# Two in-place token sums of a gate/up pass, issued behind the first pair's evictions

## The chip, the cores and the metric

The kernel runs on one core of one Trainium2 chip. The metric is the device time of one execution in microseconds (us). A profiled execution gives, beside that, a span: from the first to the last instruction of the program. The engines are TensorE (PE, the matmuls), VectorE (DVE), ScalarE (ACT), GpSimd (POOL) and SyncE (SP), which here only issues DMA transfers. Each engine works through its own queue in program order; an instruction can wait for semaphores that other engines or transfers raise, and everything behind it in its queue waits with it.

## What is computed

Two layers, each a linear-attention block and a gated MLP, on 2048 tokens of 1024 features; the MLP has 3584 inner features. The MLP, where the change lies:

```python
def _B_ref(x, w_gate, w_up, w_down):
    g = jnp.einsum("bsd,df->bsf", x, w_gate)
    u = jnp.einsum("bsd,df->bsf", x, w_up)
    h = g * u
    return jnp.einsum("bsf,fd->bsd", h, w_down)
...
x = x + _A_ref(_layernorm(x, axis=-1), A_wqkv, A_wo)
x = x + _B_ref(_layernorm(x, axis=-1), B_w_gate, B_w_up, B_w_down)
```

and the same two lines once more for the second layer, with the same weights.

## The kernel before

The MLP of a layer runs in two passes of 1024 tokens. Each has a gate/up part (`gateup`, with 14 pairs) and a down part (`down`). A pair `p` is a block of 256 inner features, once of the gate weights (unit A, `c = 0`) and once of the up weights (unit B, `c = 1`). Both units multiply a 1024x256 weight block with the tokens of the pass, and do so with seven block products instead of eight: the tokens (features by tokens, in float16) and the weights are cut into two by two blocks, sums of blocks are formed on VectorE, and products 1 to 7 of sums are added up in PSUM. One product is four matmuls of 128x128 by 128x512 (`pe`, line 1591). The token blocks that enter products 1 and 5 are `xblk(0, s0)`, a part of the normalized tokens, and the sum `T1`.

Products 1 and 5 are themselves split into seven half-size products (matmuls of 128x128 by 128x256, line 1661), from pair 1 on. Those take further sums of sub-blocks of the tokens (`tp_ops`) and of the weights (`sums0`). Four token sums belong to each of the two products. Three of them go to buffers of their own. The remaining one is formed in place: the quarter `b12` of the block is overwritten with `b22 - b12`. Pair 0 of the first layer's first pass is not split: its products 1 and 5 read the whole block, `b12` included. So in this pass the in-place sum is held back (`XD["1"]`, `XD["5"]`, line 906) until pair 0 has read the block.

What runs when is written out by hand. `ORDERS[(False, 0)]` is a list of tokens, gone through once for each pair; a `+` means the next pair, a `'` the pair before:

```python
(False, 0): "S1+ D2A M3B' P5A T1 P1B R0 P7A 57 P6B S5+ M5A D4A M2A 11+ P7B D3A 16+ D2B M4A P5B M3A R1 T0+ M2B M5B 51+ D4B P1A+ 56+ 17+ D3B P6A+ M4B",
```

`P1B` is product 1 of unit B and so on; `D2`, `D3`, `D4` are products that finish a PSUM bank. `M5A` and `M5B` evict the bank of product 5: `mul0` (line 1766) copies it on ScalarE (line 1771), and for unit B two VectorE sums follow, an addition of 128x1024 and a multiplication of 128x512. The other M tokens evict the other banks; `M4B` and `M2B` are scaled evictions on VectorE (line 843). `11`, `16`, `17` are the stages of split product 1, `51`, `56`, `57` those of split product 5: each issues half-size matmuls, then `seed` (line 1677, ScalarE) and `join` (line 1680, VectorE). `S1` and `S5` are the four weight sums for a pair's split products. `T0` and `T1` are ticks: they store weight sums and form the next ones (`prep_s`, four sums of 128x2x512), run a step of a layer norm (line 506 on VectorE, a transposing transfer at line 591 on SyncE), and every second pair `wd_load` (a load of raw down weights), `wd_prep` (its four sums of 128x1024, behind the load) and `wd_store`. `R0` and `R1` issue the load of a later weight block.

`emit` turns a token into instructions. It issues the in-place sums directly behind the last product that reads the block, `P1B` or `P5B`. All sums of this kind are recorded by `tt` at line 840, so the profile shows them under that line, and the matmuls under line 1591 or 1661. Dependencies are found by the recorder from the byte ranges that each instruction reads and writes. A matmul group of `pe` and a half-size one declare the whole token block as read.

Of the kernel before, what the change touches and what calls it, by code (L numbers as in the profile page):

```python
# [180 lines left out]
def build_kernel(nc, A_x, A_wqkv, A_wo, B_w_gate, B_w_up, B_w_down, out):  # L181
# [152 lines left out]
    with ExitStack() as es:  # L334
# [86 lines left out]
        def R(o, n):  # L421
            return [(o, o + n)]

        def r_x(i, lo=0, hi=D):
            return [(O_X + (i * D + lo) * 2, O_X + (i * D + hi) * 2)]
# [13 lines left out]
        def dma(dst_ap, src_ap, wr, key, rd=()):  # L439
            P.add("sp", lambda e: e.dma_start(dst_ap, src_ap), rd=rd, wr=wr, dma_sem=key)  # L440
# [279 lines left out]
        XD = {}  # L720
# [24 lines left out]
        def pass_base(first, ps_):  # L745
            return ps_ * (NU + len(d_units(first, 0)))
# [125 lines left out]
        def x_pop(n=1):  # L872
            for _ in range(n):
                if XQ:
                    XQ.pop(0)[1]()
# [6 lines left out]
        def x_need(tk):  # L882
            lab = X_NEED.get(tk[:2])
            while any(k == lab for k, _ in XQ):
                x_pop()
# [34 lines left out]
        def prep_s(n):  # L920
            a, b = sorted([(n + 1) % NR, (n + 2) % NR])
            ring = [f(O_SLOT, NR * SZ_SLOT // 2).rearrange("p (s x) -> p s x", s=NR)[:, a:b + 1:b - a] for f in (vb, vh)]

            def w(h, c):
                return ring[0][:, :, 1024 * h:1024 * h + 1024].rearrange("p s (k c) -> p s k c", c=256)[:, :, :, 128 * c:128 * c + 128]

            def rg(lo, hi):
                return r_slot(n, lo, hi) + r_slot(n + 1, lo, hi)
            sv = [ring[1][:, :, 2048 + 512 * i:2560 + 512 * i].rearrange("p s (k c) -> p s k c", c=128) for i in range(4)]
            a11, a12, a21, a22 = w(0, 0), w(1, 0), w(0, 1), w(1, 1)  # L930
            ra = rg(0, 4096)
            rs = [rg(4096 + i * 1024, 5120 + i * 1024) for i in range(4)]
            tt(sv[0], a21, a22, ALU.add, ra, rs[0])
            tt(sv[1], sv[0], a11, ALU.subtract, ra + rs[0], rs[1])
            tt(sv[2], a11, a21, ALU.subtract, ra, rs[2])
            tt(sv[3], a12, sv[1], ALU.subtract, ra + rs[1], rs[3])

        def store_s(n):
            u = split_n(n)[1]
            sl = (n + 1) % NR  # L940
            dma(wscr[u], vh(r_slot(n)[0][0] + 4096, 2048), R(V_S + u * 32, 32), KSW[sl], rd=r_slot(n, 4096, 8192))
# [608 lines left out]
        def pro_step(pro, n):  # L1550
            for _ in range(n):
                k = len(P.streams["pe"])
                while pro and len(P.streams["pe"]) == k:
                    pro.pop(0)()

        def layer_B(lnp, nxt, first):
# [236 lines left out]
            def gateup(ps_, ticks, l2):  # L1793
                jit = first and ps_ == 0
                NP = NU // 2
                pairs = [pair(ps_, p, "" if jit and p == 0 else l2) for p in range(NP)]

                order = ORDERS[not first, ps_].split()
                n0 = pass_base(first, ps_)

                def emit(it, tk):
                    off = {"'": -1, "+": 1}.get(tk[-1], 0)
                    tk = tk.rstrip("'+=")
                    p = it + off
                    if tk[0] == "R":
                        if it > 0 or (it == 0 and tk == "R1"):
                            ring_issue()
                        return
                    if not 0 <= p < NP:
                        return  # L1810
                    c, x = pairs[p], "AB".find(tk[-1])
                    if jit and tk[0] not in "PDMFT" and tk[-1] not in c["L"] and tk[0] not in c["L"]:
                        return
                    if p < 2:
                        x_need(tk)
                    if p == 0:
                        if tk[0] in "PDM":
                            x_pop()
                    if tk[0] == "P":
                        c["p" + tk[1]](x)  # L1820
                        if jit and p == 0 and tk in ("P1B", "P5B"):
                            XD[tk[1]]()
                    elif tk[0] == "D":
                        c["fin"](tk[1], x)
                    elif tk[0] == "M":
                        c["c22"](x) if tk[1] == "5" else c["fmul"](tk[1], x)
                    elif tk[0] == "S":
                        if jit:
                            c["sums0"](tk[1])
                        else:  # L1830
                            c["sums"](SPG[tk[1] == "5"], "make" if first else "load")
                    elif tk[0] == "F":
                        c["fold"]()
                    elif tk[0] == "T":
                        i = int(tk[1])
                        if jit:
                            if i == 0:
                                store_s(n0 + 2 * p)
                                store_s(n0 + 2 * p + 1)
                            elif p + 1 < NP:  # L1840
                                prep_s(n0 + 2 * p + 2)
                        ticks(2 * p + i)
                    else:
                        c["L"][tk[0]]["st" + tk[1]]()

                seq = [(it, tk) for it in range(-1, NP) for tk in order
                       if tk[0] == "R" or 0 <= it + {"'": -1, "+": 1}.get(tk[-1], 0) < NP]
                early = ("11", "16", "17", "P1", "21", "26", "27", "31", "36", "37", "S1", "S5", "T0", "T1", "Ra", "Rb")
                npro = [tk[:2] in early for _, tk in seq].index(False)
                if jit:  # L1850
                    npro = 1
                    seq.insert(0, seq.pop([tk for _, tk in seq].index("P1A+")))
                pro = [(lambda x=x: emit(*x)) for x in seq[:npro]]

                def tail():
                    for tk in order:
                        if tk[-1] == "'":
                            emit(NP, tk)
                    ring_issue()
                    if "Ra" in order:  # L1860
                        ring_issue()
                    for t in range(1 if jit else 3, 8):
                        i = 8 * ps_ + t
                        dma(x_res[:, i, :], xscr[i * 128:(i + 1) * 128, :], r_x(i), KX[i], rd=R(V_X + i * 32, 32))

                def run():
                    pro_step(pro, len(pro))
                    for x in seq[npro:]:
                        emit(*x)
                    return tail  # L1870
                return pro, run
# [523 lines left out]
```

## Time and profile before

| | us |
|---|---|
| median of 3 runs | 1436.92 |
| lowest and highest run | 1436.63, 1437.53 |
| the profiled execution | 1439.2 |
| its span | 1437.5 |
| gate/up of the first pass, about | 238 to 405 |

The profile is one execution. A row of its timeline has the start in us from the span's start, the duration in us, the engine and line, the operation with output and input shapes, the number of instructions merged into the row, and, in brackets, how long the engine stood idle before it and what released it. Instructions of one engine overlap a little, so rows may start before the row above has ended. All buffers lie in one SBUF tensor, `arena`, and the PSUM banks in `ps`, so names tell little and shapes and lines tell more. In the table of waits a row has the waiting instruction, whom it waited for, the total in us, the number of waits and the longest.

### The profile page before, as it was taken

What the parts mean: (1) busy time and instruction counts of PE and PEld (TensorE: products, weight loads), DVE (VectorE), ACT (ScalarE), POOL (GpSimd) and SP (SyncE); (2) the same over time, 40 slices, a digit from 0 to 9 for tenths busy, and PEclk for the clock granted to TensorE, in tenths of its full rate; (3) what the DMA queues carried; (4) which work ended last, traced back from release to release, by engine and by line L of the source; (5) the groups of instructions that cost most, each with busy time, mean ns of one, the idle gap of its engine ahead of it and who ended that gap; (6) DMA issues with size and microseconds to landing.
All of it is one profiled execution on the core that took longest, in us unless ns stands there. A gap on an engine that the chain in (4) does not pass through costs nothing.

```text
span 1437.5 us, 22075 instructions
## 1 busy us (share of the span) xinstructions
PE 1422.7 (99%) x8248; PEld 801.1 (56%) x8304; DVE 1141.0 (79%) x2048; ACT 700.3 (49%) x1478; POOL 226.0 (16%) x265
## 2 busy tenths in 40 slices
PE   9999999999999999999999999999999999999999
PEld 4444444555544555554664444456666477666548
DVE  7878887889857799877678878879877787777856
ACT  4752357677720255550156523567776016777401
POOL 4643632000000000000034346300000000000000
PEclk9999999999999999999999999999999999999999
DMA  7416868987889899996898077679976699787558
GB/s 235 107 25 194 173 139 201 255 294 255 292 304 336 259 271 295 277 276 228 248 363 207 30 185 156 148 222 274 284 257 198 225 295 319 256 265 256 205 165 240
DMA packets 386667, 331.05 MB, mean 230 GB/s; under 512 B 178432, under 2 KB 333952, under 8 KB 386048
## 3 DMA queue, kind: packets, MB, share of 16 engines
q1 hardware_dynamic: 386560, 329.64, 76.9%
q8 instruction: 65, 1.06, 0.3%
q14 instruction: 42, 0.34, 0.1%
HBM read 241.24 MB, written 64.75 MB: 213 GB/s over the span
## 4 chain that ended last, share of the span: by engine, by line
PE 92%; DVE 3%; DMA 2%; ACT 1%; issue 1%; SPq 1%; POOL 0%; DVEq 0%
PE ps L1591 25%; PE ps L1661 17%; PE ps L2163 16%; PE ps L1400 8%; PE ps L1498 6%; PE ps L1166 6%; PE ps L2058 6%; PE ps L970 5%; PE ps L980 3%; DVE arena L840 2%; DMA arena<-in_A_wqkv_dram 1%; DMA arena<-in_B_w_down_dram 1%; SPq L440 1%; PE ps L1412 0%; PE ps L1440 0%
## 5 line engine op out<-in xcount | busy, mean ns | idle before, releaser
L840 DVE TENSOR_TENSOR arena<-arena 128x512 f16<-128x512 f16 (+9 forms) x776 | 429.9, 581 | 77.0 <-ACT arena L1705 45.1
L1591 PE MATMUL ps<-arena 128*128 128x512 f16 x1808 | 446.8, 379 | 0.6 <-ACT ps L1621 0.6
L843 DVE SCALAR_TENSOR_TENSOR arena<-ps,arena 128x512 f16<-128x512 f32 (+2 forms) x440 | 293.8, 686 | 76.1 <-PE ps L2163 48.3
L1661 PE MATMUL ps<-arena 128*128 128x256 f16 x2324 | 312.1, 273 | 3.7 <-DVE arena L840 1.6
L1661 PEld LDWEIGHTS ps<-arena 128*128 128x128 f16 (+1 forms) x2324 | 226.2, 98 | 107.6 <-DVE ps L1680 5.2
L1591 PEld LDWEIGHTS ps<-arena 128*128 128x128 f16 (+1 forms) x1808 | 176.6, 98 | 141.6 <-ACT ps L1621 1.1
L2163 PE MATMUL ps<-arena 128*128 128x512 f16 (+1 forms) x1053 | 229.9, 379 | 0.6
L1596 ACT ACTIVATE arena<-ps 128x512 f16<-128x512 f32 x224 | 133.9, 598 | 91.5 <-PE ps L1591 89.4
L2163 PEld LDWEIGHTS ps<-arena 128*128 128x128 f16 x1064 | 104.1, 98 | 124.7
L1677 ACT COPY ps<-ps 128x256 f32<-128x256 f32 x220 | 81.1, 369 | 131.4 <-PE ps L1661 122.9
L1680 DVE TENSOR_TENSOR ps<-ps,arena 128x256 f32<-128x256 f32 x220 | 92.3, 428 | 36.5 <-PE ps L1661 19.4
L1400 PE MATMUL ps<-arena 128*128 128x512 bf16 x499 | 114.1, 379 | 0.7
L2062 ACT COPY ps<-ps 128x256 f32<-128x256 f32 x36 | 12.9, 357 | 204.9 <-PE ps L2058 204.9
L1498 PE MATMUL ps<-arena 128*128 128x512 bf16 x500 | 110.7, 379 | 0.6
L483 POOL TENSOR_SCALAR arena<-arena 128x1 f32<-128x1 f32 x43 | 16.4, 380 | 591.5 <-DVE arena L482 591.5
L2058 PE MATMUL ps<-arena 128*128 128x256 f16 (+1 forms) x882 | 97.8, 273 | 0.1
L1166 PE MATMUL ps<-arena 128*128 128x512 bf16 (+1 forms) x412 | 94.7, 379 | 0.8 <-DVE ps L1170 0.3
L2058 PEld LDWEIGHTS ps<-arena 128*128 128x128 f16 x882 | 85.7, 98 | 11.9 <-DVE arena L843 0.7
L1306 POOL TENSOR_TENSOR arena<-arena 128x1024 f16<-128x1024 f32 x32 | 79.2, 2474 | 70.1 <-DVE arena L1304 61.6
L1621 ACT COPY ps<-ps 128x512 f32<-128x512 f32 x112 | 64.2, 573 | 50.6 <-PE ps L1661 44.8
L1005 POOL TENSOR_TENSOR arena<-arena 128x512 f32<-128x512 f32 x60 | 73.5, 1243 | 69.4 <-DVE arena L1095 33.7
L1498 PEld LDWEIGHTS ps<-arena 128*128 128x128 f16 x512 | 50.1, 98 | 59.8
(78 smaller groups left out, 1223.5 us busy)
## 6 DMA issues: line engine op xcount, KB each, us to landing
arena<-w_scratch SPq DMA_DIRECT2D x84, 512.0 KB, 5.2
arena<-sp_scratch SPq DMA_DIRECT2D x56, 512.0 KB, 6.0
arena<-t_scratch SPq DMA_DIRECT2D x29, 896.0 KB, 6.4
arena<-in_B_w_down_dram SPq DMA_DIRECT2D x20, 896.0 KB, 7.3
w_scratch<-arena SPq DMA_DIRECT2D x28, 512.0 KB, 6.0
sp_scratch<-arena SPq DMA_DIRECT2D x28, 512.0 KB, 4.2
arena<-in_B_w_gate_dram SPq DMA_DIRECT2D x42, 256.0 KB, 5.2
arena<-in_B_w_up_dram SPq DMA_DIRECT2D x42, 256.0 KB, 3.3
```

What stands on the lines that cost most here:

```text
L840: P.add("dve", lambda e: e.tensor_tensor(out=out, in0=a, in1=b, op=op), rd=rd, wr=wr, prd=prd)
L843: P.add("dve", lambda e: e.scalar_tensor_tensor(out=out, in0=a, scalar=sc, in1=b, op0=ALU.mult, op1=op1), rd=rd, wr=wr, prd=prd)
L1166: P.add("pe", lambda e: [e.matmul(psb(bank), x[:, k, :], w[:, k, :], start=(start and k == 0), stop=(k == 3), skip_group_check=True) for k ...
L1400: return [e.matmul(psb(bank), xr[:, t, j * 128:(j + 1) * 128], pk[:, h, t, :], start=(t == 0), stop=(t == NST - 1)) for t in range(NST)]
L1498: return [e.matmul(psb(bank), xnT[:, g, i * 128:(i + 1) * 128], wp[:, g, dh * 512:(dh + 1) * 512], start=(dh == 0 and g == 0), stop=(g == ...
L1591: P.add("pe", lambda e: [e.matmul(psb(bank), w[:, k, :], x[:, k, :], start=(start and k == 0), stop=(k == 3), skip_group_check=True) for k ...
L1596: P.add("act", lambda e: e.activation(t, psb(bank), AF.Copy, scale=SG), prd=[bank], wr=r)
L1661: P.add("pe", lambda e: [e.matmul(psb(bank)[:, 256 * half:256 * half + 256], w[:, k, :], xx[:, k, :], start=(start and k == 0), stop=(k == ...
L1677: P.add("act", lambda e: e.copy(psb(dst[c])[:, 0:256], lo), prd=[bk], pwr=[dst[c]])
L1680: P.add("dve", lambda e: e.tensor_tensor(out=psb(dst[c])[:, 256:512], in0=lo, in1=c5, op=ALU.add), prd=[bk], rd=rc5, pwr=[dst[c]])
L2058: P.add("pe", lambda e: [e.matmul(psb(bank)[:, 256 * half:256 * half + 256], a[:, k, :], w[:, k, :], start=(start and k == 0), stop=(k == ...
L2163: return [e.matmul(psb(bank), hv[:, 7 * hf + k, t * 128:(t + 1) * 128], w[:, k, :], start=(start and hf == 0 and k == 0), stop=(hf == 1 an ...
```

## The change

The two in-place sums are no longer issued behind `P1B` and `P5B` but behind the evictions `M5A` and `M5B` of pair 0: the sum for product 1 with `M5A` (x = 0), that for product 5 with `M5B` (x = 1).

```diff
                     if tk[0] == "P":
                         c["p" + tk[1]](x)
-                        if jit and p == 0 and tk in ("P1B", "P5B"):
-                            XD[tk[1]]()
                     elif tk[0] == "D":
                         c["fin"](tk[1], x)
                     elif tk[0] == "M":
                         c["c22"](x) if tk[1] == "5" else c["fmul"](tk[1], x)
+                        if jit and p == 0 and tk[1] == "5":
+                            XD["15"[x]]()
```

In VectorE's queue, where pair 0 runs into pair 1, the first of the two (the 128x2x256 sum, which waits for P1B by `s_pe`) stands directly behind a layer-norm step (L506). The four sums of 128x256 are `S5` of pair 1:

```order
 L506 TENSOR_SCALAR arena<-arena 128x1024 [waits d_tl0,s_pool]
+L840 TENSOR_TENSOR arena<-arena 128x256
+L840 TENSOR_TENSOR arena<-arena 128x256 [waits s_dve]
+L840 TENSOR_TENSOR arena<-arena 128x256
+L840 TENSOR_TENSOR arena<-arena 128x256 [waits s_dve]
 L840 TENSOR_TENSOR arena<-arena 128x2x256 [waits s_pe]
-L840 TENSOR_TENSOR arena<-arena 128x256
-L840 TENSOR_TENSOR arena<-arena 128x256 [waits s_dve]
-L840 TENSOR_TENSOR arena<-arena 128x256
-L840 TENSOR_TENSOR arena<-arena 128x256 [waits s_dve]
```

The sum now stands behind the four weight sums instead of ahead of them; the eviction `M5A` has no VectorE instruction.

A few rows on in the same queue is the second one. Before, from the join of token 16 (L1680) to the joins of 56 and 17; the four 128x1024 sums that begin with the wait for `d_dr` are `wd_prep`, L843 is the eviction `M2B`, and the 128x1024 and 128x512 sums behind it are `M5B`:

```order
L1680 TENSOR_TENSOR ps<-ps,arena 128x256 [waits s_pe]
L840 TENSOR_TENSOR arena<-arena 128x2x256 [waits s_pe]
L840 TENSOR_TENSOR arena<-arena 128x1024 [waits d_dr]
L840 TENSOR_TENSOR arena<-arena 128x1024 [waits s_dve]
L840 TENSOR_TENSOR arena<-arena 128x1024
L840 TENSOR_TENSOR arena<-arena 128x1024 [waits s_dve]
L843 SCALAR_TENSOR_TENSOR arena<-ps,arena 128x512
L840 TENSOR_TENSOR arena<-arena 128x1024 [waits s_act]
L840 TENSOR_TENSOR arena<-arena 128x512 [waits s_dve]
L1680 TENSOR_TENSOR ps<-ps,arena 128x256 [waits s_pe]
```

and now:

```order
L1680 TENSOR_TENSOR ps<-ps,arena 128x256 [waits s_pe]
L840 TENSOR_TENSOR arena<-arena 128x1024 [waits d_dr]
L840 TENSOR_TENSOR arena<-arena 128x1024 [waits s_dve]
L840 TENSOR_TENSOR arena<-arena 128x1024
L840 TENSOR_TENSOR arena<-arena 128x1024 [waits s_dve]
L843 SCALAR_TENSOR_TENSOR arena<-ps,arena 128x512 [waits s_pe]
L840 TENSOR_TENSOR arena<-arena 128x1024 [waits s_act]
L840 TENSOR_TENSOR arena<-arena 128x512 [waits s_dve]
L840 TENSOR_TENSOR arena<-arena 128x2x256
L1680 TENSOR_TENSOR ps<-ps,arena 128x256 [waits s_pe]
```

The sum for product 5 has gone from ahead of `wd_prep` to behind `M5B`, past seven instructions, and its wait for PE is now taken by the instructions ahead of it.

PE's queue keeps its order. Where token 51 begins (the first row, which waits for VectorE) and `D4B` follows (L1591), one wait for ScalarE is gone, since the wait of token 51 now covers it:

```order
 L1661 MATMUL ps<-arena 128x256 [waits s_dve]
 L1661 MATMUL ps<-arena 128x256 x3
-L1591 MATMUL ps<-arena 128x512 [waits s_act]
-L1591 MATMUL ps<-arena 128x512 x3
+L1591 MATMUL ps<-arena 128x512 x4
 L1661 MATMUL ps<-arena 128x256 x4
```

POOL's and SyncE's queues are the same as before, and ScalarE's keeps its order and drops waits that others cover.

## The prediction

> **What bounds the kernel now.** The page first: its row of busy times, and the head of the chain that ended last.
>
> ```profile
> PE 1422.7 (99%) x8248; PEld 801.1 (56%) x8304; DVE 1141.0 (79%) x2048; ACT 700.3 (49%) x1478; POOL 226.0 (16%) x265
> PE 92%; DVE 3%; DMA 2%; ACT 1%; issue 1%; SPq 1%; POOL 0%; DVEq 0%
> ```
>
> TensorE (PE) is busy for 1422.7 of 1437.5 us. The change adds no matmul and takes none away, so it can act only through the moments at which PE stands still. Next I read the table of waits, for PE, over 235 to 251 us, where the first gate/up pass of layer one begins, and then over the rest of the run.
>
> ```profile
> PE ps L1661 <- DVE arena L840: 1.6, 2, 1.1
> PE ps L1591 <- ACT ps L1621: 0.6, 1, 0.6
> ...
> PE ps L1661 <- DVE ps L1680: 1.4, 1, 1.4
> PE ps L970 <- DMA arena<-in_A_wqkv_dram: 0.9, 1, 0.9
> PE ps L1661 <- ACT arena L1705: 0.6, 2, 0.4
> ```
>
> The first row is two waits of the half-size products (L1661) for VectorE sums (DVE L840). The last three rows are all that PE waits for after 251 us: 2.9 us. The timeline of PE shows the two places of the first row, and which products stand there.
>
> ```profile
> 242.84 1.90 PE L1591 MATMUL ps<-arena 128*128 128x512 f16 x8 [0.58 <-ACT ps L1621]
> 245.81 0.61 PE L1661 MATMUL ps<-arena 128*128 128x256 f16 x4 [1.06 <-DVE arena L840]
> 246.25 1.89 PE L1591 MATMUL ps<-arena 128*128 128x512 f16 x8
> 247.98 0.38 PE L1661 MATMUL ps<-arena 128*128 128x256 f16 x2
> 248.20 1.89 PE L1591 MATMUL ps<-arena 128*128 128x512 f16 x8
> 250.61 0.61 PE L1661 MATMUL ps<-arena 128*128 128x256 f16 x4 [0.52 <-DVE arena L840]
> 251.92 1.04 PE L1661 MATMUL ps<-arena 128*128 128x256 f16 x8
> ```
>
> By the token order, the four half-size matmuls at 245.81 are token 11 of the second pair, the four at 250.61 its token 51, and the eight at 248.20 end with P5B. VectorE at the same moments (the two first rows are cut out by narrow windows):
>
> ```profile
> 245.33 0.42 DVE L840 TENSOR_TENSOR arena<-arena 128x512 f16<-128x512 f16 x1
> 245.66 1.02 DVE L840 TENSOR_TENSOR arena<-arena 128x256 f16<-128x256 f16 x4
> 248.40 0.43 DVE L1680 TENSOR_TENSOR ps<-ps,arena 128x256 f32<-128x256 f32 x1 [1.72 <-PE ps L1661]
> 250.13 2.96 DVE L840 TENSOR_TENSOR arena<-arena 128x512 f16<-128x512 f16 x5 [1.29 <-PE ps L1591]
> 253.00 0.69 DVE L843 SCALAR_TENSOR_TENSOR arena<-ps,arena 128x512 f16<-128x512 f32 x1
> 253.60 1.14 DVE L840 TENSOR_TENSOR arena<-arena 128x1024 f16<-128x1024 f16 x2
> 254.66 0.76 DVE L1680 TENSOR_TENSOR ps<-ps,arena 128x256 f32<-128x256 f32 x2
> ```
>
> The 0.42 us row at 245.33 is the in-place sum for product 1. It ends at 245.75 and token 11 starts at 245.81, so PE waits for just this sum, 0.06 us away. The group at 250.13 is the in-place sum for product 5 and then the four 128x1024 sums that prepare down weights (`wd_prep`). It waited 1.29 us for P5B to end (248.20 + 1.89 = 250.09), and token 51 follows it. Both moved instructions are thus the last thing PE waits for, before and after. No other wait hides them.
>
> **The first sum.** It moves behind four sums of 128x256. From the rows, they last 1.02 us together, and neighbours overlap by 0.09 (245.33 + 0.42 against 245.66), so the sum starts 0.94 later and token 11 at 246.75. PE has nothing to do meanwhile: its eight matmuls from 242.84 end at 244.74. What sat ahead of it as a wait (P1B) was long over, since P1B stands before those eight. **Cost 0.94 us**, and the wait of 1.06 becomes 2.0.
>
> **The second sum.** Up to P5B everything on PE is now 0.94 late, so P5B ends at 251.03. VectorE's join of 248.40 goes to 249.34 and its successor can start at 249.68 (0.43 less the overlap). That successor is now `wd_prep`, which waits for the first raw down weights. Their load, issued at 240.22, has landed long before:
>
> ```profile
> 240.22 0.64 SPq L440 DMA_DIRECT2D arena<-in_B_w_down_dram  x1
> arena<-in_B_w_down_dram SPq DMA_DIRECT2D x1, 1024.0 KB, 7.1
> ```
>
> Then, in start-to-start times of the rows above: four `wd_prep` sums 2.54 (253.00 - 250.13 - 0.33 for the sum that stood ahead), the scaled eviction 0.60, the two evictions' sums of M5B 1.06. Their input from ScalarE is the copy at 250.13, 0.60 long, which comes 0.94 later and so by 251.67, no obstacle. The moved sum starts at 249.68 + 2.54 + 0.60 + 1.06 = 253.88, ends at 254.30, and token 51 goes at 254.36 and not at 250.61. **PE is 3.75 us late** there, of which 0.94 came from the first sum; its own wait grows from 0.52 to about 3.3. The 1.29 us that VectorE no longer idles does not help PE, because PE's next input stands at the end of that work.
>
> **What is given back.** The 1.4 us wait for L1680 comes next. The chain that ended last shows where it is from:
>
> ```profile
> 258.63 1.90 DVE arena L840 x3
> 260.94 0.43 SPq L440
> 267.29 8.52 DMA arena<-in_B_w_down_dram
> 275.84 0.70 DVE arena L840
> 280.12 0.35 DVE ps L1680
> 280.52 0.83 PE ps L1661 x6
> ```
>
> The weight sums that end at 260.53 release stores on SyncE's queue; behind these, in the same queue, stands the second load of raw down weights (267.29), then its `wd_prep` on VectorE, and behind it the join for which PE waits at 280.52. PE's last work before:
>
> ```profile
> 276.35 2.75 PE L1591 MATMUL ps<-arena 128*128 128x512 f16 x12
> ```
>
> It ends at 279.10, so without the wait the next matmul could go at 278.94 (matmuls overlap by some 0.16: 246.25 + 1.89 against the next group's 247.98). The slack is 1.58 us. How late is this chain itself? It hangs on VectorE, and VectorE on these:
>
> ```profile
> 254.72 0.60 ACT L1596 ACTIVATE arena<-ps 128x512 f16<-128x512 f32 x1 [0.59 <-PE ps L1591]
> 255.22 0.59 ACT L1771 ACTIVATE arena<-ps 128x512 f16<-128x512 f32 x1
> 255.92 4.61 DVE L840 TENSOR_TENSOR arena<-arena 128x256 f16<-128x256 bf16 x10
> 256.85 0.69 DVE L840 TENSOR_TENSOR arena<-arena 128x1024 f16<-128x1024 f16 x1
> ```
>
> The 128x1024 sum at 256.85 needs the copy of 255.22, which follows one that waits for PE. Both come 3.75 later, so the copy ends at 259.56 and the sum starts at 259.59: 2.74 late. VectorE itself is there earlier: PE's matmuls before the joins (the eight at 251.92) end near 256.7, a ScalarE copy of 0.36 and the remaining work bring it to about 259.1. From there the chain runs on without PE: SyncE's issues, the load and `wd_prep` move by 2.74, the load lands at 278.55, and PE goes at 283.26, while it was ready at 278.94 + 3.75 = 282.69. VectorE, with its work up to the load at most 3.75 late, does not come in between, for it idled 2.11 us:
>
> ```profile
> 275.84 2.62 DVE L840 TENSOR_TENSOR arena<-arena 128x1024 f16<-128x1024 bf16 x4 [2.11 <-DMA arena<-in_B_w_down_dram]
> ```
>
> So a wait of about 0.4 us remains, 1.0 us is given back, and **the sum is 3.75 - 1.01 = 2.74 us**. Behind 283 us PE had no wait in this pass; the later waits (0.9 and 0.6) follow transfers and copies that PE itself releases, and I let them move along at nothing. If that cover failed they could only shrink.
>
> The bounds come from the load. In this pass the first and third loads took 7.1 and 6.8 us against 8.52 for the second:
>
> ```profile
> arena<-in_B_w_down_dram SPq DMA_DIRECT2D x1, 1024.0 KB, 6.8
> ```
>
> If it lands over 0.57 us sooner, no wait is left and the loss is 3.75 - 1.58 = 2.17. It may also land later, because a load that PE releases draws near the stores (3.75 late against 2.74):
>
> ```profile
> 259.04 0.38 SPq L440 DMA_DIRECT2D arena<-in_B_w_up_dram  x1
> ```
>
> Against that, the gate load behind it, released by PE too, competes later. I keep 2.74, since the same queue holds the same transfers, and 2.17 to 3.4 as the forecast's own bounds.
>
> **Rivals.** (a) Nothing is given back: the second load lands a full 1.0 us later than reckoned, and the wait moves along with PE. For it speaks the crowding just named; against it, that the competing gate load gives way by as much. Loss 3.75: 1440.7 us.
>
> (b) The clock. The first matmuls of the program, on a PE that had done nothing, ran at half pace:
>
> ```profile
> L447 PE MATMUL ps<-arena 128*128 128x512 f16 x10 | 4.1, 593 | 1.4 <-POOL arena L443 1.4
> ```
>
> Ten in 4.1 us, against twelve in 2.75 at 276.35. PE never stood still for over 1.4 us after that; the new wait is 3.3. Should it bring the slow pace back for as long as at the start, some eight matmuls lose 0.2 each, 1.7 us: PE is ready at 284.4, past the chain's 283.26, and the loss is 3.87: 1440.8 us. Against it: nothing here shows how long an idle stretch must be. The Trainium skill ("TensorE: Matmul & The Clock Gate", Part 1) has such a rule: one idle window of about 3.4 us halves the clock, and about 3.4 us of work restores it. By that rule 3.3 us just misses, and the time would stay at the sum. The same page's table under "Why this matters for your kernels" is stricter and wants no gap over about 3 us; by that the 3.87 would come. No run so far shows which holds.
>
> (c) Not slower: the whole loss runs into later slack. If the 1.58 and the other two waits (0.9, 0.6) vanish, 0.7 us stays: 1437.6. It decides at the load of the second layer's weights: it would have to be issued independently of PE, and in a stage where PE frees the buffers that is unlikely.
>
> (d) The change does not do what it says: token 51 does not wait for the moved sum. Then PE can go there at 250.87 (250.09 - 0.16 + 0.94), 0.26 later than before; VectorE comes out of its block 0.45 earlier (254.21 against 254.66), the chain to 280.52 with it, and the time is 1436.5, no change. Against it: the product reads the whole block that the sum writes into, and its wait for VectorE stands in both orders.
>
> **How the numbers follow.** The profiled execution took 1439.2 us for its span of 1437.5; the median of the runs shown is 1436.92, 2.3 lower, with 1437.53 as the highest. I put the loss on the median: 1436.92 + 2.74 = 1439.7. Chances: forecast 0.59, (a) 0.17, (b) 0.10, (c) 0.07, (d) 0.05, and 0.02 for a gain that I cannot name. The bound of 0.2%, about what a measurement of this kernel tells from no change, is 2.87 us, so the forecast lies across it: own range 1439.1 to 1440.3, and I count 0.35 of its chance above and 0.24 below. Slower: 0.35 + 0.17 + 0.10 = 0.62. Same: 0.24 + 0.07 + 0.05 = 0.36. Faster: 0.02. The range takes in (a) and (b) with the runs' scatter of 0.6 and leaves out (c) and (d): 1438.6 to 1441.4.
>
> **What would show it.** In the changed kernel's waits, PE's two waits for L840 should sum to about 5.3 us, the longer one 3.3, with matmuls at 246.75 and 254.36; VectorE should start `wd_prep` at 249.7 without a wait; PE's wait for L1680 should shrink from 1.4 to about 0.4 near 283, and PE's work behind it stand 2.7 later. Wrong would be: a second long wait near 283 (then (a)), 128x512 matmuls 0.4 apart behind 254 (then (b)), the two waits unchanged (then (d)), or a smaller shift at the end than at 283 (then (c)).

## The result, and the profile after

The changed kernel took 1443.64 us (median of 5 runs, 1443.30 to 1444.39) against 1436.92 (median of by now 5 runs, 1436.63 to 1437.53): ratio 1.004, 95% interval 1.0029 to 1.0051. Beside other runs of before, on two more occasions, it was 1442.47 against 1438.11 (1.0025, 1.0014 to 1.0036) and 1442.73 against 1438.08 (1.0033, 1.0022 to 1.0045). So it is slower by 4.4 to 6.7 us, where 2.7 was forecast and 1441.4 was the upper end of the range. The kernel before itself measured 1436.92 on the first occasion and 1438.1 on the two others.

PE's busy time and its waits from 235 us on, in the first profiled execution of the changed kernel (span 1442.7):

```profile
PE 1428.2 (99%) x8304; PEld 802.0 (56%) x8304; DVE 1141.6 (79%) x2048; ACT 700.3 (49%) x1478; POOL 225.7 (16%) x265
...
PE ps L1661 <- DVE arena L840: 5.3, 2, 3.3
PE ps L1661 <- DVE ps L1680: 0.8, 1, 0.8
PE ps L1661 <- ACT arena L1705: 0.6, 2, 0.4
PE ps L1591 <- ACT ps L1621: 0.6, 1, 0.6
```

The two waits for L840 sum to 5.3 us, as forecast. The wait for L1680 has shrunk from 1.4 to 0.8, not to the 0.4 of the forecast. PE's busy time, 5.5 us above before's, cannot be compared: the profile of before holds 8248 matmul records and this one 8304. The timeline of PE over the two places:

```profile
244.45 1.90 PE L1591 MATMUL ps<-arena 128*128 128x512 f16 x8 [0.58 <-ACT ps L1621]
248.33 0.61 PE L1661 MATMUL ps<-arena 128*128 128x256 f16 x4 [1.98 <-DVE arena L840]
250.72 1.89 PE L1591 MATMUL ps<-arena 128*128 128x512 f16 x8
255.93 0.61 PE L1661 MATMUL ps<-arena 128*128 128x256 f16 x4 [3.32 <-DVE arena L840]
256.38 1.59 PE L1591 MATMUL ps<-arena 128*128 128x512 f16 x4
257.76 1.91 PE L1661 MATMUL ps<-arena 128*128 128x256 f16 x8
259.46 3.08 PE L1591 MATMUL ps<-arena 128*128 128x512 f16 x12
262.38 0.82 PE L1661 MATMUL ps<-arena 128*128 128x256 f16 x6
```

Everything is 1.6 us later to begin with: the eight matmuls ahead of the first gap stood at 242.84 before. From there to token 51 it took 255.93 - 244.45 = 11.48 us, before 250.61 - 242.84 = 7.77: a delay of 3.71. Behind token 51 the same groups take longer: four matmuls 1.59 us (1.03 before), eight half-size ones 1.91 (1.04). From 255.93 to the six matmuls at 262.38 it is 6.45 us, before 255.38 - 250.61 = 4.77 (the start of that group of six in before's timeline), so another 1.68. The view by windows names the reason. Its columns are the stretch, its length, the busy time of each engine (with the number of instructions), the granted clock of PE, the share of busy DMA engines and GB/s; the stretches are cut where the clock changes, and one such length ahead:

```profile
246.46:249.87 3.41, 1.54 (x10) 0.90 (x11) 1.78 (x7) 1.31 (x5) 0.00 (x0) 1.00 0.96 347
249.87:253.29 3.42, 2.74 (x14) 1.15 (x12) 2.33 (x5) 2.14 (x4) 0.00 (x0) 1.00 1.16 293
253.29:256.70 3.41, 0.77 (x6) 0.60 (x7) 2.55 (x5) 0.12 (x1) 0.00 (x0) 1.00 0.93 344
256.70:260.11 3.41, 3.41 (x14) 1.76 (x12) 0.45 (x2) 1.45 (x4) 0.00 (x0) 0.50 0.23 64
```

For 3.41 us PE ran at half clock, after a stretch of 3.41 us in which it was busy for 0.77. Half a window of full-speed work is lost: 1.7 us. A stretch of 3.41 us at half clock is called a cold window below.

The 1.6 us at the start are not the change's doing: in this execution the clock also fell once at the very beginning. The first matmuls of the program behind the layer norm, after the change:

```profile
7.54 1.89 PE L980 MATMUL ps<-arena 128*128 128x512 bf16 x4 [0.46 <-ACT arena L599]
9.22 1.06 PE L605 MATMUL ps<-arena 128*128 128x128 f16 x8
```

and, with the columns of the view by windows, the stretches around them:

```profile
4.11:7.53 3.42, 1.55 (x12) 0.65 (x10) 2.56 (x6) 0.63 (x2) 0.98 (x3) 1.00 0.99 342
7.53:10.94 3.41, 3.40 (x15) 1.69 (x16) 2.14 (x4) 1.07 (x2) 0.83 (x3) 0.50 1.09 359
```

In before the same matmuls took:

```profile
7.41 1.04 PE L980 MATMUL ps<-arena 128*128 128x512 bf16 x4 [0.45 <-ACT arena L599]
8.73 0.62 PE L605 MATMUL ps<-arena 128*128 128x128 f16 x8 [0.28 <-DVE arena L513]
```

VectorE did what the new order says. Its timeline after the change:

```profile
246.93 1.35 DVE L840 TENSOR_TENSOR arena<-arena 128x256 f16<-128x256 f16 x5
250.92 0.43 DVE L1680 TENSOR_TENSOR ps<-ps,arena 128x256 f32<-128x256 f32 x1 [2.65 <-PE ps L1661]
251.27 2.61 DVE L840 TENSOR_TENSOR arena<-arena 128x1024 f16<-128x1024 bf16 x4
253.79 0.68 DVE L843 SCALAR_TENSOR_TENSOR arena<-ps,arena 128x512 f16<-128x512 f32 x1
254.40 1.48 DVE L840 TENSOR_TENSOR arena<-arena 128x1024 f16<-128x1024 f16 x3
259.28 0.43 DVE L1680 TENSOR_TENSOR ps<-ps,arena 128x256 f32<-128x256 f32 x1 [3.41 <-PE ps L1661]
```

`wd_prep` follows the join without a wait, and the last of the three sums from 254.40 is the moved one: it ends at 255.88, and token 51 goes at 255.93. What VectorE gained by not waiting for P5B it idles away behind it (3.41 us). The chain of the second load of down weights, which ended near 280 before:

```profile
262.21 0.60 ACT arena L1771
...
273.74 8.40 DMA arena<-in_B_w_down_dram
...
286.45 0.35 DVE ps L1680
286.85 0.83 PE ps L1661 x6
```

The ScalarE copy at 262.21 is the one that stood at 255.22 before. Less the 1.61 us of the start it is 5.38 late, as PE is: 3.71 from the two sums and 1.68 from the cold window, which lies ahead of it. The load behind it is 273.74 - 267.29 - 1.61 = 4.84 late, where 2.74 was forecast. So a wait of 0.75 us is left at 286.85, and the change costs 286.85 - 280.52 - 1.61 = 4.72 us there.

### The profile page after: what moved, and what is told of

It reads as the page before. It is cut to its first block, busy times and chain, and to the rows that moved or that the text cites. A ratio compares the mean times of both kernels' runs of the same rounds, so it can differ in the third digit from the quotient of the medians.

```text
span 1442.7 us, 22129 instructions
## 1 busy us (share of the span) xinstructions
PE 1428.2 (99%) x8304; PEld 802.0 (56%) x8304; DVE 1141.6 (79%) x2048; ACT 700.3 (49%) x1478; POOL 225.7 (16%) x265
## 4 chain that ended last, share of the span: by engine, by line
PE 88%; DVE 7%; DMA 2%; ACT 1%; SPq 1%; issue 1%; POOL 0%; DVEq 0%; POOLq 0%
PE ps L1591 25%; PE ps L1661 17%; PE ps L2163 16%; PE ps L2058 6%; PE ps L1498 6%; PE ps L1166 6%; PE ps L970 5%; PE ps L1400 4%; PE ps L980 3%; DVE arena L840 2%; DVE arena L1297 1%; DVE arena L1300 1%; DMA arena<-in_B_w_down_dram 1%; DMA arena<-arena 1%; SPq L440 0%
## 5 line engine op out<-in xcount | busy, mean ns | idle before, releaser
L840 DVE TENSOR_TENSOR arena<-arena 128x512 f16<-128x512 f16 (+9 forms) x776 | 429.7, 580 | 76.5 <-ACT arena L1705 45.1
L1591 PE MATMUL ps<-arena 128*128 128x512 f16 x1808 | 447.8, 380 | 0.6 <-ACT ps L1621 0.6
L843 DVE SCALAR_TENSOR_TENSOR arena<-ps,arena 128x512 f16<-128x512 f32 (+2 forms) x440 | 293.5, 685 | 75.6 <-PE ps L2163 48.0
L1591 PEld LDWEIGHTS ps<-arena 128*128 128x128 f16 (+1 forms) x1808 | 176.7, 98 | 142.2 <-ACT ps L1621 1.1
L1680 DVE TENSOR_TENSOR ps<-ps,arena 128x256 f32<-128x256 f32 x220 | 92.3, 428 | 42.2 <-PE ps L1661 24.6
```

What stands on the lines that cost most here:

```text
L840: P.add("dve", lambda e: e.tensor_tensor(out=out, in0=a, in1=b, op=op), rd=rd, wr=wr, prd=prd)
L843: P.add("dve", lambda e: e.scalar_tensor_tensor(out=out, in0=a, scalar=sc, in1=b, op0=ALU.mult, op1=op1), rd=rd, wr=wr, prd=prd)
L1591: P.add("pe", lambda e: [e.matmul(psb(bank), w[:, k, :], x[:, k, :], start=(start and k == 0), stop=(k == 3), skip_group_check=True) for k ...
L1680: P.add("dve", lambda e: e.tensor_tensor(out=psb(dst[c])[:, 256:512], in0=lo, in1=c5, op=ALU.add), prd=[bk], rd=rc5, pwr=[dst[c]])
```

## The experiments

Theory C says that the loss beyond the two gaps comes from the clock of PE. Its rivals: K, that the delays cost more through transfers further on; S, that the profiled execution of before or the first measurement was not typical; E, that VectorE's new order costs by itself. A run's mean clock of 0.999 is read below as one cold window (half of 3.41 in 1437 us is 0.0012), 0.998 as two. The slow first matmuls of the program are not counted in it: the profiled execution of before has them and a mean of 1.000. The reading is not exact, since a fall at the very end of the program counts as well, and a cold window need not lie at the two gaps: of the 30 runs of before on the second occasion five had 0.999, of 32 in the first set of experiments two, of 28 on the third occasion none. Times of one group were taken beside the same runs of before.

**Before once more** (no edit).

> The kernel before, once more, for a second trace of it. Theory S (the profiled execution of before was not typical): its 1.4 us wait for L1680 near 280 us and its 0.9 us wait for the second layer's key weights belong to a slow moment of the transfers; here they are shorter or gone, together under 1 us, and the time is 1436 to 1438 us. Rival (the waits are the kernel's own): both waits are there again with 1.2 to 1.6 and 0.7 to 1.1 us.

Measured: 1438.48 us against 1438.03 (1.0002, 0.9993 to 1.0011); 3 of 11 runs at 0.999. The wait near 280 is 1.2, where the first trace had 1.4, and the one for the second layer's weights is gone:

```profile
PE ps L1661 <- DVE arena L840: 1.5, 2, 1.0
PE ps L1661 <- DVE ps L1680: 1.2, 1, 1.2
```

So the wait that the forecast counted on to be given back is in both traces; the 0.9 us one is in one of the two. Neither side had it wholly right.

**Only the sum for product 5 moved.**

```diff
-                        if jit and p == 0 and tk in ("P1B", "P5B"):
+                        if jit and p == 0 and tk == "P1B":
                             XD[tk[1]]()
...
                         c["c22"](x) if tk[1] == "5" else c["fmul"](tk[1], x)
+                        if jit and p == 0 and tk == "M5B":
+                            XD["5"]()
```

> Only the sum for product 5 is moved (behind M5B); the one for product 1 stays behind P1B. PE's wait at token 11 is 1.06 us as in before, that at token 51 stays at 3.3 us, since VectorE and PE are both 0.94 us earlier. Theory C (the 3.3 us wait brings the slow clock for one window): the slow stretch is there, and the time is 0.9 us below the changed kernel, 1442.6 us. Rival K (the loss beyond 3.75 us is made by both delays together further on, by transfers): no slow stretch is needed, and the time falls by more than 2 us, to under 1441.6.

Measured: 1442.10 us against 1438.03 (1.0025, 1.0016 to 1.0034); 9 of 11 runs with a clock below 1.000. The trace has the gap of 3.3 us, the slow stretch behind it, and no wait for L1680 near 280 at all. The time lies between the 1442.6 of theory C and K's bound of 1441.6; the slow stretch decides for C: one gap alone is enough for the clock.

**Twelve matmuls in the second gap.**

```diff
-                        c["L"][tk[0]]["st" + tk[1]]()
+                        warm() if jit and p == 1 and tk == "51" else None; c["L"][tk[0]]["st" + tk[1]]()
```

where `warm` issues the twelve matmuls described here:

> The changed kernel, with twelve more matmuls of 128x512 on PE just ahead of token 51, into the bank that token 51 begins anew (their result is not used): 2.6 us of work inside the 3.3 us gap. Theory C: no slow stretch of the clock behind 254 us, token 51 starts when it did, and the time falls by 1.7 us to about 1441.9. Rival K: the clock plays no part in the time, it stays within 0.3 us of the changed kernel's 1443.6.

Measured: 1442.57 us (1.0029, 1.0019 to 1.0038), not the 1441.9 expected, and 6 of 10 runs below 1.000. The time lies between what theory C and rival K asked for and decides nothing; the four runs at 1.000 took 1440.50 to 1442.77 and do not stand apart from the others either. The trace shows why the gain was missed: behind token 51 there is no slow stretch, but there is one earlier, behind the gap of 2.0 us at token 11:

```profile
244.67:248.08 3.41, 1.43 (x10) 0.68 (x8) 2.79 (x8) 1.57 (x3) 0.33 (x1) 1.00 1.01 338
248.08:251.49 3.41, 3.41 (x10) 1.23 (x9) 0.00 (x0) 1.73 (x4) 0.00 (x0) 0.50 1.15 336
```

PE was idle for 1.98 of the first 3.41 us. A whole idle window is not needed; the gap of token 11, which the forecast had not considered for the clock, can do it.

**The sum for product 5 behind M2B.**

```diff
-                        if jit and p == 0 and tk[1] == "5":
+                        if jit and p == 0 and tk in ("M5A", "M2B"):
                             XD["15"[x]]()
```

> The sum for product 1 as in the change, the sum for product 5 issued behind M2B, ahead of the two sums of M5B: 1.07 us earlier on VectorE, so the gap on PE is 2.25 us and the delay at token 51 is 2.7 us. Theory C with a gap of about 3 us or more needed: no slow stretch, time 2.8 us below the changed kernel (1.07 and 1.7), 1440.9. Theory C with a shorter gap sufficing: slow stretch there, 1.1 us below, 1442.6. Rival K: 1.1 us below without a slow stretch.

Measured: 1441.51 us (1.0021, 1.0012 to 1.0029). The runs fall apart by clock: the three at 1.000 took 1439.66 to 1440.61, the eight at 0.999 took 1441.16 to 1443.19. The median lies between theory C's two values, 1440.9 and 1442.6: with gaps of 1.98 and 2.25 us a cold window comes or not, from run to run. The profiled run is one of the three at 1.000, and its trace has no slow stretch behind either gap.

**The changed kernel again** (no edit).

> The changed kernel once more, for a second trace and for times beside the runs of the same session. Theory C, now sharper: one window of 3.4 us with much idle PE time in it, not a whole idle one, halves the clock for the next window; the 3.3 us gap does it always, the 2.0 us gap at token 11 only where a window happens to hold nearly all of it. Expected: 3.75 us of delay, 1.7 for each cold window, about 1.2 given back near 280, so 4.2 us over before with one cold window and 5.9 with two; a time of 1442.2 to 1444, and runs with a mean clock of 0.998 slower than those with 0.999 by 1.7. Rival S (the 6.7 us of the first measurement are real and more than gaps and clock): 6 us or more over before.

Measured: 1442.47 us (1440.30 to 1444.85), 4.4 over before (1.0025, 1.0014 to 1.0036). Seven of eight runs were below 1.000. The one at 1.000 took 1440.30, the four at 0.999 took 1442.10 to 1442.55, and the three lower ones 1443.13 to 1444.85. Its trace has two cold windows, one behind each gap:

```profile
243.57:246.98 3.41, 1.38 (x8) 0.41 (x6) 3.31 (x9) 1.58 (x3) 0.84 (x1) 1.00 0.97 286
246.98:250.40 3.42, 3.42 (x11) 1.53 (x12) 0.00 (x0) 1.29 (x4) 0.00 (x0) 0.50 1.09 367
250.40:253.81 3.41, 2.52 (x13) 1.06 (x11) 2.54 (x5) 1.63 (x3) 0.00 (x0) 1.00 1.13 335
253.81:257.22 3.41, 0.98 (x7) 0.70 (x8) 2.34 (x5) 0.33 (x2) 0.00 (x0) 1.00 0.33 135
257.22:260.64 3.42, 3.42 (x14) 1.81 (x12) 0.87 (x3) 1.24 (x4) 0.00 (x0) 0.50 0.34 98
```

In this trace the join behind the second load comes 6.55 us later than before, counted from the eight matmuls ahead of the first gap (287.27 - 243.04 against 280.52 - 242.84).

**Only the sum for product 1 moved.** The edit mirrors the one for product 5: `XD["1"]()` behind `M5A`, `XD["5"]()` left at `P5B`.

> Only the sum for product 1 is moved (behind M5A); that for product 5 stays behind P5B. Gap of 2.0 us at token 11, 0.5 at token 51, delay 0.95 us. Theory C: in part of the runs a cold window (clock 0.999), those 1.7 us slower than the rest; the delay alone is absorbed by the 1.2 us wait near 280, so runs without one equal before within 0.3 us, and the median lies 0 to 1.7 us over before. Rival (clock drops need a gap near 3.4 us): no cold windows, within 0.3 us of before.

Measured: 1439.38 us against 1438.11 (1.0006, 0.9998 to 1.0015). Four of 11 runs at 0.999, on average 1440.25; the seven at 1.000 on average 1438.58: 1.67 us apart, the price of one window. Five of the 30 runs of before beside them had 0.999 too, so not all four need be the gap's doing. The seven lie 0.47 over before, a little more than the 0.3 expected. The profiled run was one of the seven, and it gives the other side of the threshold:

```profile
244.80:248.21 3.41, 1.46 (x9) 0.89 (x10) 1.86 (x7) 1.35 (x4) 0.00 (x0) 1.00 1.01 365
248.21:251.63 3.42, 2.90 (x16) 1.25 (x14) 1.00 (x3) 2.14 (x4) 0.00 (x0) 1.00 1.16 268
```

1.95 us idle, and the clock stayed.

**Both gaps filled.** As above, but `warm` is called ahead of both tokens:

```diff
-                        c["L"][tk[0]]["st" + tk[1]]()
+                        warm(tk[0], {"1": 7, "5": 12}[tk[0]]) if jit and p == 1 and tk in ("11", "51") else None; c["L"][tk[0]]["st" + tk[1]]()
```

> The changed kernel with both gaps of PE filled: seven more matmuls ahead of token 11 (1.5 of 2.0 us) and twelve ahead of token 51 (2.6 of 3.3 us), into the banks that these tokens begin anew; results not used. Theory C: no cold window in any run (clock 1.0), and only the delay is left: 3.75 less the 1.2 given back, 2.5 us over before. Rival S: the time stays at the changed kernel's.

Measured: 1440.83 us against 1438.11 (1.002, 1.0011 to 1.0029), that is 2.72 us over before (1.6 to 4.2 by the interval), where 2.5 was expected. Nine of 11 runs were at 1.000; two were not, about as many as in before's own runs. The waits that are left in its trace, and the clock over the whole place:

```profile
PE ps L1661 <- DVE arena L840: 1.2, 2, 0.7
...
PE ps L1661 <- DVE ps L1680: 0.5, 1, 0.5
```

```profile
245.00:262.00 17.00, 15.82 (x86) 8.15 (x85) 11.24 (x27) 7.67 (x17) 0.00 (x0) 1.00 0.75 236
```

The products wait for VectorE as in the changed kernel: tokens 11 and 51 start 3.85 and 11.46 us behind the start of the eight matmuls ahead of the first gap, there 3.88 and 11.48. Only PE is kept busy meanwhile. This is the change without its clock: 2.7 us. With the clock, beside the same runs of before, it is 4.4.

**Narrow reads.** The half-size products declare only the quarter that they read:

```diff
-                    b11, b12, b21, b22 = [(x[:, 2 * k:2 * k + 2, 256 * c:256 * c + 256], rx) for k in range(2) for c in range(2)]
+                    qb, qp = (O_T, 1024) if q == "5" else (rx[0][0], S * 2); b11, b12, b21, b22 = [(x[:, 2 * k:2 * k + 2, 256 * c:256 * c + 256], _seg(qb + 2 * k * qp, 2, qp, 512 * c, 512 * c + 512)) for k in range(2) for c in range(2)]
```

First in the changed order:

> The changed order, but the half-size products declare only the quarter of the token block that they read, so tokens 11 and 51 no longer wait for the in-place sum of another quarter. Theory D (all of the loss comes from those two waits of PE): both gaps vanish, no cold window, and the time is not above before; worked out from before's rows, PE is 1.6 us earlier at token 51, the chain through the second load of down weights moves with the ScalarE copies by as much, so 1.0 to 1.6 us under before. Rival E (VectorE's order itself costs, by what now stands behind wd_prep): still over before by more than 1 us.

Measured: 1435.86 us against 1438.11 (0.9983, 0.9974 to 0.9991); one of 11 runs at 0.999. The whole loss has turned into a gain, with VectorE's order untouched: rival E falls, and the loss comes from the two waits of PE. The gain is larger than worked out.

**The sum for product 5 directly behind wd_prep**, that for product 1 left at `P1B`:

```diff
                         ticks(2 * p + i)
+                        if jit and p == 1 and i == 0:
+                            XD["5"]()
```

> The sum for product 1 stays behind P1B; the sum for product 5 goes only behind wd_prep, ahead of M2B and M5B. From before's rows VectorE reaches it at 251.28 us, so the gap on PE is 1.67 us and the delay at token 51 is 1.15 us. Theory C with a threshold near 1.95 us of idle time within one 3.4 us window (1.95 brought no cold window in one trace, 1.98 and 2.03 did): no cold window in any run, clock 1.0 throughout apart from the start, and the delay vanishes in the 1.2 us wait near 280, so the time equals before within 0.4 us. If the threshold lies lower than 1.6: cold windows in part of the runs and a median 0.5 to 1.7 over before.

Measured: 1438.45 us against 1438.08 (1.0004, 0.9995 to 1.0013); 10 of 11 runs at 1.000. The stretch with its gap, and the next:

```profile
249.74:253.15 3.41, 1.75 (x12) 0.80 (x9) 3.38 (x7) 1.24 (x3) 0.00 (x0) 1.00 1.10 276
253.15:256.57 3.42, 3.42 (x21) 1.96 (x20) 2.59 (x8) 1.47 (x4) 0.00 (x0) 1.00 1.02 362
```

1.66 us idle, no cold window, and the delay is swallowed by the wait near 280, as expected.

**Narrow reads in the order of before, the changed order with narrow reads again, and the changed kernel a third time**, on one chip.

> The order of before with the narrow reads. Theory D: the gaps at tokens 11 and 51 are gone as in the changed order with narrow reads; but VectorE still waits for P5B ahead of wd_prep, so the chain through the second load of down weights moves by 1.06 us, not by 1.6: 1.0 us under before, about 1437.1 beside a before of 1438.1, and 0.5 us to 1 us over the changed order with narrow reads. Rival: it equals the changed order with narrow reads within 0.3 us, so the order of the two sums no longer matters at all.

> The changed order with narrow reads once more, beside e_narrow_before and on the same chip: 1435.9 with a before of 1438.1, 1.6 to 2.3 us under before, no cold windows.

> The changed kernel a third time, on whatever chip comes. Theory C: 4.4 us over before as in the second measurement, plus or minus 1, most runs with a mean clock of 0.999, runs without a cold window (1.000) about 2.5 over before. If the 6.7 us of the first measurement is what the kernel costs and the second measurement was the exception: over 6 us.

Measured, against 1438.08: 1436.42 us in the order of before (0.9987, 0.9978 to 0.9996), 1435.04 in the changed order (0.998, 0.9971 to 0.9989), 1442.73 for the changed kernel, none of its six runs at 1.000. With narrow reads the changed order is the better one, by 1.4 us here. The first measurement of it, 1435.86, was 2.25 below its own before, only 0.6 more than the 1.66 of the order of before. Expected were 1.0 for the order of before and 0.5 to 1 between the two orders, so both came out larger. Here are `wd_prep` on VectorE, the second load of down weights on SyncE's queue, and two rows of PE, first in the order of before:

```profile
249.60 2.96 DVE L840 TENSOR_TENSOR arena<-arena 128x512 f16<-128x512 f16 x5 [1.29 <-PE ps L1591]
...
266.49 0.59 SPq L440 DMA_DIRECT2D arena<-in_B_w_down_dram  x1
...
243.56 1.90 PE L1591 MATMUL ps<-arena 128*128 128x512 f16 x8 [0.58 <-ACT ps L1621]
254.62 0.83 PE L1661 MATMUL ps<-arena 128*128 128x256 f16 x6 [0.29 <-DVE ps L1680]
```

then in the changed one:

```profile
247.43 2.61 DVE L840 TENSOR_TENSOR arena<-arena 128x1024 f16<-128x1024 bf16 x4
...
264.57 0.63 SPq L440 DMA_DIRECT2D arena<-in_B_w_down_dram  x1
...
242.77 1.90 PE L1591 MATMUL ps<-arena 128*128 128x512 f16 x8 [0.58 <-ACT ps L1621]
253.38 0.82 PE L1661 MATMUL ps<-arena 128*128 128x256 f16 x6
```

VectorE no longer stands 1.29 us for P5B, and the load goes 1.9 us sooner; but 0.79 of that is there ahead of the pass already (243.56 against 242.77), where the order is the same. What the order does on PE is seen between its two rows: 11.06 us before, 10.61 now, because the join no longer makes PE wait 0.29, and groups that follow without a wait overlap by 0.16 here (250.79 + 2.75, the group ahead, against 253.38). That is 0.45 of the 1.50 us by which the two spans (1434.4 and 1432.9) differ; some 0.2 more is a wait for the second layer's weights, which only the order of before has. So the traces show about a third of the difference as the order's. That all of the 1.4 us between the medians comes from it is not shown.

The long wait near 280 is in neither of these two traces, though 0.5 us of it stands in the first trace of the changed order with narrow reads. The expectation of 1.0 to 1.6 let the chain move along with PE, and so left that wait in; where it is gone, the gain is larger.

## Why the prediction was wrong

**The two moved sums** were right. The waits at tokens 11 and 51 were forecast as 2.0 and 3.3 us and were 1.98 and 3.32; the delay at token 51 as 3.75 and was 3.71.

**What is given back** was right in kind. With the gaps filled, the time is 2.72 us over before, where the sum said 2.74; that it is so close is luck, for the interval reaches from 1.6 to 4.2. In single traces the wait near 280 shrank to 0.5 (gaps filled) or vanished (third trace of the changed kernel, and the one with the sum for product 5 alone).

**The failing step is rival (b), the clock,** which the sum put at nothing with a chance of 0.10. Its price for one window, 1.7 us, was right (1.68 in the trace, 1.67 between runs), and so was the sign that would show it. Three things were not.

First, the chance: 18 of 19 runs of the changed kernel had a mean clock below 1.000, and its three traces have four cold windows behind the two gaps. It was weighed by the length of one gap against one window, "By that rule 3.3 us just misses". The Trainium skill ("TensorE: Matmul & The Clock Gate", Part 1) has a free-running window of some 3.4 us, an idle one that halves the clock and a busy one that restores it. The traces agree in the window: 3.41 us, on one fixed grid through an execution (in the first trace of the changed kernel the cold windows at 7.53 and 256.70 are 73 lengths of 3.413 us apart), and the clock is back after one busy window. But the window needs not be idle. Over all windows around the two gaps, in the ten traces without narrow reads in which a change of the clock shows where the grid lies (the one with the sum behind M2B shows none), those with 1.95 us idle or less left the clock alone, and those with 1.98 or more halved it for the next window. The Trainium skill ("TensorE: Matmul & The Clock Gate", "Why this matters for your kernels") has a stricter row, no gap above about 3 us; it came nearer, and is still too generous. Nor is the figure of 1.96 us the whole of it: at the start of the program the window from 4.11, with 1.87 idle, was followed by a cold one. What was counted differently there is open.

Second, the number of windows: (b) had one, behind token 51. The gap of token 11 can bring another, as in the second trace, where the loss at the join is 6.55 us.

Third, (b) let PE lose 1.7 us alone and the chain go on at 283.26, so that the whole wait near 280 was given back and 3.87 us remained. By (b) as it stood the time would have been 1440.8, inside the range. In the first trace the chain was held up by the cold window too, a wait of 0.75 was left, and the loss there is 4.72. In the third trace the load took 7.7 us and not 8.4, no wait was left, and the loss is 3.90 (284.49 - 242.91 against 280.52 - 242.84).

Since the window runs free, its place against a gap is a matter of chance. A gap of `g` us, if it is longer than 1.96, holds 1.96 idle us of some window in a share of (3.41 + g - 3.92) / 3.41 of all places (estimated from the threshold above): 0.43 for 1.98 us, 0.51 for 2.25, 0.82 for 3.32; a gap of 1.66 never does. Seen, as runs below 1.000: 4 of 11 for the first sum alone, 9 of 11 for the second alone, 8 of 11 for 1.98 and 2.25 together, 1 of 11 with 1.66. Beside those, before itself had 0 to 3 in 11, so the agreement is rough. So the change costs 2.7 us and, most often, one or two windows of 1.7, of which a little is given back too.

**Rivals (a), (c) and (d)** did not come. With the gaps filled the load's wait shrank, so (a) falls; nothing was absorbed beyond that wait, so (c) falls; the waits grew as the order says, so (d) falls. Yet (d) had its point: it is only the whole-block read that makes the products wait for a sum they do not use.

**What stays open.** The first comparison gave 6.7 us, the two others 4.4 and 4.7; 1.2 us of the difference lie in the kernel before, which was faster on the first occasion. The first trace of the changed kernel carries one cold window at the start of the program, which is not the change's. Why its three runs with a clock of 0.999 took 1443.3 to 1443.7 us, and not mostly 1442.0 to 1442.6 as later, and one with 0.997 no more than these, was not settled; the intervals of the three ratios overlap between 1.0029 and 1.0036.

## What to carry to other kernels

Where the matmul engine is the bound, price a new gap twice: by its own length, and by the clock, if the idle time within some 3.4 us can reach 2 us. Then ask what else hangs on the matmuls in the slow stretch. An in-place update belongs directly behind its last reader when something waits for the buffer; work of 4 us in between shows up as a gap on the engine that waits, even if the engine that runs it gets busier and idles less. And look at what a recorder believes is read: with reads declared by quarter, the same order of instructions went from 4.4 us slower than before to 2 or 3 us faster.

## What was not expected of the hardware

One window of 3.41 us with PE busy for 1.43 us was followed by one at half clock, one with 1.46 us busy was not. So runs of one program can lie a window's price apart: 1438.58 and 1440.25 on average with only the first sum moved. Other scatter of the runs is about as large. A comparison of kernels at this scale has to look at the clock of each run beside its time.
